# Tiles 4 to 8 of a pooled-attention and expert kernel in the form of the later tiles

## The chip, the cores and the metric

The kernel runs on one core of one Trainium2 chip. The metric is the device time of one execution in microseconds; the time before is the median of three runs. All engine times come from one profiled execution.

## The reference

Attention with pooled keys and values feeds a mixture of four experts. Batch is 8, heads 8, sequence 576, head size 64.

```python
k_p = k.reshape(B, H, Sp, 8, D).mean(axis=3)      # 576 rows -> 72
v_p = v.reshape(B, H, Sp, 8, D).mean(axis=3)
scores = scale * np.matmul(q, k_p.transpose(0, 1, 3, 2))
attn = exp(scores - max) / (sum + 1e-09)
x = np.matmul(attn, v_p)                          # -> x: 4608 tokens x 512
p = domain_probs / (domain_probs.sum(-1, keepdims=True) + 1e-09)
for e in range(4):
    out += p[:, e:e+1] * (np.maximum(x @ w1[e], 0.0) @ w2[e])   # 512 -> 1024 -> 512
```

## The kernel before

The 4608 tokens are 36 tiles of 128 tokens, and four tiles are a group. The expert part runs over 36 steps, one for each group and expert. A step has twelve slots. In every three slots there are two blocks of `up` (L807, a 128 x 512 product block of the next step, four products each, with a Relu on ScalarE) and one `down` (L843, one tile of this step, eight products, and `collect` on VectorE). `up` fills one of two `h_ps` banks, `down` one of two `o_ps` banks. Step 0 has only its last `down`, in slot 11; tiles 0 to 3 are prepared before slot 0 in an order written out by hand.

The attention of the later tiles is laid between these products. A dictionary `plan` holds, for a slot number counted through all steps, the functions that are called when the slot's products have been issued. Within an engine the order of the program is the order of the work. So this plan decides what each engine does next, and a wait at the head of an engine holds everything behind it.

Before the change the tiles come in two forms.

- **Tiles 4 to 8** (`plan_tile`): `gather_q` (L195) picks a tile's queries out of the wide load `qrun`; `turn_q` turns them with four 128 x 128 transposes on TensorE (L512); `scores` (L555) is four products against `kT`, in which the keys of a pair of heads lie beside blocks of zeros; `less_max` (VectorE) subtracts the row's maximum; `expo` (ScalarE) takes the exponential into `e_sb`; `normalise` (VectorE) divides; `turn_e` turns the probabilities with five transposes (L512); `context_turned` (L753) is eight products against `vblk`, in which the values are spread beside zeros.
- **Tiles 9 to 35** (`plan_pair`): queries and probabilities are turned on VectorE in blocks of 32; `scores_by_quarters` (L580) and `context_by_quarters` (L772) use products of 64 x 64, four of which address the four quarters of TensorE's array. These products are put into the middle of a `down`: the dictionary `parted` names the slots, and there six of eight products come first, then the block, then the last two.

Keys and values are folded from eight rows to one on VectorE (`fold_k`, `end_k`, `fold_v`, `end_v`). `WB = 2` says that batches 0 and 1 have the layout with zeros (`kTs`, `vblks`). From batch 2 on, `kTh` and `vh` hold them without zeros, and `spread_v` fills the part of `vh` that the last eight of a head's 72 rows need. Loads that convert to bf16 are issued on GpSimd (POOL), in program order, with eight semaphores in turn: an issue waits until the load eight before it has landed. Float32 loads and the output's stores are issued on SyncE (SP).

PSUM has two `ps_h` banks, two `ps_o` banks, one double bank `ps_s` (`sc`) and two `ps_t` banks for turns and contexts.

Of the kernel before, what the change touches and what calls it, by code (L numbers as in the profile page):

```python
# [10 lines left out]
ALU = mybir.AluOpType  # L11
# [6 lines left out]
def kernel(  # L18
# [33 lines left out]
    PW = 2 * SP  # L52

    WB = 2
# [62 lines left out]
    def load_k(b):  # L117
        if b < KB:
            load_rows(nc.gpsimd, kraw[b % 2], rows_of(k[b]))
            return  # L120

        n, mid = HR // 2, HR // 2 // BLK
        odd = n - mid * BLK
        for n32 in range(P // BLK):
            y, half = divmod(n32, 2)
            p0 = n32 * BLK
            for g in range(2):
                head = 4 * g + 2 * y
                rows = k[b][head:head + 2, :, half * BLK:(half + 1) * BLK].rearrange(
                    "z (j r) d -> (z j) r d", r=POOL  # L130
                )

                r = odd * g
                parts = [(r + a * BLK, r + (a + 1) * BLK) for a in range(mid)]
                parts.append((0, odd) if g else (n - odd, n))
                for r0, r1 in parts:
                    a, i = divmod(g * n + r0, BLK)
                    nc.gpsimd.dma_start(  # L138
                        out=k_blocks(b)[p0 + i:p0 + i + r1 - r0, a].rearrange(
                            "i (r d) -> i r d", d=BLK  # L140
                        ),
                        in_=rows[r0:r1],
                    )

    def load_v(b):
        if b < WB:
            load_rows(nc.gpsimd, vraw[b % 2], rows_of(v[b]))
            return


        if b < WB + 2:
            nc.gpsimd.memset(vraw[b % 2][0:TAIL, NB - 1, :], 0.0)
        rows = v[b].rearrange("(g y z) (j r) d -> g z j y (r d)", g=2, y=2, r=POOL)
        to = vraw[b % 2][:].rearrange("p (c y) x -> p c y x", y=2)
        for g in range(2):
            for z in range(2):
                p0 = g * D + z * REST
                nc.gpsimd.dma_start(out=to[g * D:(g + 1) * D, z], in_=rows[g, z, 0:D])  # L158
                nc.gpsimd.dma_start(out=to[p0:p0 + REST, 2], in_=rows[g, z, D:SP])  # L159
# [10 lines left out]

# [22 lines left out]
    def gather_q(t):  # L193
        qrow[t] = qpool.tile([P, NPAIR, 2, D], BF16, name="qrow")
        nc.vector.tensor_copy(  # L195
            out=qrow[t][:],
            in_=qrun[:, :, :, t - TPG - 1, :].rearrange("p z c d -> p c z d"),
        )

    def load_qblk(b):  # L200

        qblk[b] = qbpool.tile([P, NPAIR * (S // BLK), BLK], BF16, name="qblk")
        for n32 in range(P // BLK):
            y, half = divmod(n32, 2)
            to = qblk[b][n32 * BLK:(n32 + 1) * BLK].rearrange("i (g c) d -> i g c d", g=2)
            for g in range(2):
                head = 4 * g + 2 * y
                nc.gpsimd.dma_start(  # L208
                    out=to[:, g],
                    in_=q[b][head:head + 2, :, half * BLK:(half + 1) * BLK]  # L210
                    .rearrange("z (a i) d -> i (z a) d", i=BLK),
                )
# [63 lines left out]

    after(k0[0:1, 1, POOL * D - 1:POOL * D])
# [6 lines left out]
    load_q(TPG)  # L284
    load_w1(2, (0,))
    load_w2(1, halves)
    load_q_wide()
# [7 lines left out]
    vblks = [raw.tile([P, NB, NZ, D], BF16, name=f"vblk{i}") for i in range(2)]  # L295
    nc.scalar.memzero(vraw[0][TAIL:P, NB - 1, :])
    for t in (vraw[1], *kraw):
        nc.scalar.memzero(t[TAIL:P, NB - 1, :])
    kTs = [raw.tile([P, ROWS], BF16, name=f"kT{i}") for i in range(2)]
    for t in kTs:  # L300
        nc.scalar.memzero(t[:])
    for t in vblks:
        nc.scalar.memzero(t[:, :, 0])
# [87 lines left out]
    def turn_k(b):  # L391

        flat = pads[b][:].rearrange("p i z d -> p (i z d)")
        ps = ps_t.tile([P, NB * P], BF16, tag="t", name="kT_ps")
        for i in range(NB):

            nc.tensor.transpose(
                ps[:, i * P:(i + 1) * P], flat[:, i * P:(i + 1) * P], ident[:]
            )
        kT[b] = kTs[b % 2] if b < WB else kTh[b % 2]  # L400
        copy = nc.scalar.copy
        for z in range(2):
            half = slice(z * D, (z + 1) * D)
            if b >= WB:
                copy(
                    out=kT[b][half].rearrange("x (g r) -> x g r", g=2),
                    in_=ps[half, 0:ROWS].rearrange("x (g y r) -> x y g r", g=2, y=2)[:, z],
                )
                continue
            copy(  # L410
                out=kT[b][half].rearrange("x (c z j) -> x z c j", z=2, j=SP)[:, z],
                in_=ps[half, 0:ROWS].rearrange("x (z c j) -> x z c j", z=2, j=SP)[:, z],
            )
# [28 lines left out]
    def end_k0(*copies):  # L442
        kT[0] = kTs[0]
# [7 lines left out]
    vsum = {}  # L451

    def fold_v(b, n):
        fold(vraw[b % 2], 0, NB if b < WB else NB + 1, n)

    def end_v(b):
        rows = vraw[b % 2]
        if b >= WB:
            vblk[b] = vh[b % 2]
            nc.vector.tensor_add(  # L460
                out=vblk[b][:, 0:3].rearrange("p c y d -> p (c y) d"),
                in0=rows[:, :, 0:D], in1=rows[:, :, D:2 * D],
            )
            return
        vsum[b] = prep.tile([P, NB, D], BF16, name="v_sum")
        nc.vector.tensor_add(
            out=vsum[b][:], in0=rows[:, 0:NB, 0:D], in1=rows[:, 0:NB, D:2 * D]
        )

    def spread_v(b):  # L470
        if b >= WB:

            nc.vector.tensor_tensor(
                out=vblk[b][:, 3:5],
                in0=vblk[b][:, 2].unsqueeze(1).to_broadcast([P, 2, 2, D]),
                in1=mask_r[:].unsqueeze(2).to_broadcast([P, 2, 2, D]), op=ALU.mult,
            )
            return
        vblk[b] = vblks[b % 2]
        nc.vector.tensor_tensor(  # L480
            out=vblk[b][:, :, 1:NZ],
            in0=vsum[b][:].unsqueeze(2).to_broadcast([P, NB, MZ, D]),
            in1=mask_v[:], op=ALU.mult,
        )

# [10 lines left out]
    def spread_part(b, i0, i1):  # L496
        vblk[b] = vblks[b % 2]
# [63 lines left out]
    def scores_by_quarters(t, apart):  # L561


        if apart:

            banks = [ps_h.tile([P, 512], F32, tag="h", name="scq")[:] for _ in range(2)]
            ds[t] = soft.tile([P, 2, 4, SP], F32, name="d_sb")
        else:
# [3 lines left out]
        for pair in range(NPAIR):  # L572
            g, z = divmod(pair, 2)
            at = (2 * z + g) * SP
            for i in range(2):

                half, b = slice(i * D, (i + 1) * D), (t * P + i * D) // S
                for y in range(2):
                    dims = slice(y * D, (y + 1) * D)
                    nc.tensor.matmul(  # L580
                        banks[y][half, at:at + SP], lhsT=qT[t][dims, pair, half],
                        rhs=kT[b][dims, pair * SP:(pair + 1) * SP],
# [42 lines left out]
    def expo(t):  # L625
# [6 lines left out]
        if t >= DT:  # L632
# [21 lines left out]
    def normalise(t):  # L654
# [4 lines left out]
        if t >= DT:  # L659
# [100 lines left out]
    def context_by_quarters(tiles):  # L760
# [3 lines left out]
        banks = [ps_t.tile([P, n, 2, P], F32, tag="t", name="xT_ps") for _ in range(2)]  # L764
# [17 lines left out]
        for g in range(2):  # L782
            nc.scalar.copy(  # L783
                out=dst[:, 2 * g:2 * g + 2].rearrange("p y (c x) -> p y c x", c=n),
                in_=banks[g][:].rearrange("p c y x -> p y c x"),
            )

    def by_quarters(done, t, apart):

        if apart:  # L790
            scores_by_quarters(apart, True)
        if t:
            scores_by_quarters(t, False)
        if done:
            context_by_quarters(done)
# [115 lines left out]
    def plan_tile(t, base, steps):  # L911
        at(base, turn_q, t)
        at(base + steps[0], scores, t)
        at(base + steps[0], less_max, t)
        at(base + steps[1], expo, t)
        at(base + steps[2], normalise, t)
        at(base + steps[3], turn_e, t)
        at(base + steps[4], context_turned, t)
        return base + steps[4] + 1
# [4 lines left out]
    def plan_pair(slot, done, tiles, turns, second):  # L924

        parted[slot] = (done, tiles[0], tiles[1] if len(tiles) > 1 else None)
# [11 lines left out]
    plan_batch(1, 3, 4, 5, 7, 18, 19, 20, 21)  # L938
    for t in range(TPG, 2 * TPG):
        assert plan_tile(t, 12 + 3 * (t - TPG), (3, 5, 6, 9, 11)) <= 3 * SLOTS - 2  # L940
    for t in range(TPG + 1, DT):
        at(t + 8, gather_q, t)
    due = DT - 1 - TPG
    assert plan_tile(DT - 1, due * SLOTS - 14, (2, 4, 5, 8, 10)) <= due * SLOTS
    slot = due * SLOTS - 1
    plan_batch(2, *(slot + x for x in (-7, -6, -5, -3, 1, 2, 3, 4)))
    plan_pair(slot, [], [DT, DT + 1], (slot - 2, slot - 1), slot + 9)
# [15 lines left out]
    parted[(NT - 1 - TPG) * SLOTS - 4] = (done, None, None)  # L963
# [10 lines left out]
    for i in range(2):  # L974
        nc.scalar.memzero(vraw[i][:, NB, :])
# [91 lines left out]
    zeros = [x for i in range(2) for x in (ehalf[i][:, 2 * P:], eTh[i][:, 2])]  # L1067
    for i, x in enumerate(zeros):
        at(SLOTS + 3 * i + 2, nc.scalar.memzero, x)
# [5 lines left out]
    for s in range(NSTEP):  # L1075
        for slot in range(SLOTS):
# [6 lines left out]
            elif s > 0 or i == TPG - 1:  # L1083
                n = s * SLOTS + slot
                if n in parted:

                    down(s, i, 0, FB - 2)
                    by_quarters(*parted.pop(n))
                    down(s, i, FB - 2)
# [36 lines left out]
```

## Time and profile before

| | |
|---|---|
| median of three runs | 543.76 us (543.41 to 544.13) |
| profiled execution | 543.71 us |
| its span | 542.0 us |
| granted TensorE clock | 1.000 |
| TensorE busy | 534.3 us (99%), 3626 products |
| VectorE busy | 391.1 us (72%) |
| ScalarE busy | 236.2 us (44%) |
| GpSimd busy | 200.4 us (37%) |
| start of slot 0 | 32.12 us |
| start of the `down` of slot 47 | 88.00 us |

Busy times are shares of the whole span. In the timeline of an engine a line gives the start, the busy time, the engine, the source line, the operation, the tiles as out<-in, the part of the array, the shape and the count. Products are pipelined, so a group's busy time overlaps the next group's start; the difference of two starts is the time that a group takes on the engine.

### The profile page before, as it was taken

How to read it: one execution, taken by the hardware profiler on the slowest of the kernel's cores; microseconds unless marked ns; L12 is line 12 of the kernel's file. 1: busy time of each engine (PE TensorE's matmuls, PEld its weight loads, DVE VectorE, ACT ScalarE, POOL GpSimd, SP SyncE). 2: the span in 40 equal slices, each digit the busy share in tenths (PEclk: the TensorE clock that was granted, in tenths of full speed). 3: DMA queues.
4: the chain of work that ended last, by engine and by line, in shares of the span. 5: the costliest groups of instructions: out<-in, count | busy, mean ns of one | idle time of the engine just before them, and what ended most of it. 6: DMA issues, size and time to landing. Idle time of an engine off the chain costs nothing.

```text
span 542.0 us, 9291 instructions
## 1 busy us (share of the span) xinstructions
PE 534.3 (99%) x3626; PEld 258.4 (48%) x3626; DVE 391.1 (72%) x969; ACT 236.2 (44%) x423; POOL 200.4 (37%) x338
## 2 busy tenths in 40 slices
PE   7999999999999999999999999999999999999997
PEld 5754554444444444444444444444444444444444
DVE  5846846997979687888979797979797968522223
ACT  7444655344344444435344544354434444333330
POOL 6253299999996002991099422000000000000000
PEclk9999999999999999999999999999999999999999
DMA  9999999696979012793169949001000100011002
GB/s 228 207 201 205 191 109 106 35 56 33 113 47 88 2 46 38 29 58 61 59 26 41 68 88 37 0 1 59 21 0 1 59 21 0 2 39 40 0 1 78
DMA packets 135052, 33.78 MB, mean 62 GB/s; under 512 B 112544, under 2 KB 129952, under 8 KB 135008
## 3 DMA queue, kind: packets, MB, share of 16 engines
q0 software_dynamic: 122928, 21.45, 53.9%
q1 hardware_dynamic: 12080, 11.74, 6.7%
q8 instruction: 28, 0.46, 0.4%
q14 instruction: 16, 0.13, 0.1%
HBM read 45.16 MB, written 9.44 MB: 101 GB/s over the span
## 4 chain that ended last, share of the span: by engine, by line
PE 95%; DVE 2%; DMA 1%; ACT 1%; issue 1%; SPq 0%
PE o_ps L843 45%; PE h_ps L807 44%; PE h_ps L824 1%; PE xT_ps L772 1%; DMA qg<-in_q_dram 1%; PE scq L580 1%; PE xT_ps L753 0%; PE sc L580 0%; PE eT_ps L512 0%; PE last_ps L876 0%; PE sc L555 0%; DVE d_sb L606 0%; DVE ebuf L676 0%; SPq L109 0%; PE qT_ps L512 0%
## 5 line engine op out<-in xcount | busy, mean ns | idle before, releaser
L811 ACT ACTIVATE h_sb<-h_ps 128x512 bf16<-128x512 f32 x280 | 167.1, 597 | 247.3 <-PE h_ps L807 247.0
L843 PE MATMUL o_ps<-w,h_sb 128*128 128x512 bf16 x1144 | 272.4, 379 | 0.0
L807 PE MATMUL h_ps<-xT,w 128*128 128x512 bf16 x1120 | 265.7, 379 | 0.0
L843 PEld LDWEIGHTS <-h_sb 128*128 128x128 bf16 x1144 | 110.5, 98 | 131.8
L807 PEld LDWEIGHTS <-w 128*128 128x128 bf16 x1120 | 108.9, 98 | 128.5 <-issue 0.2
L858 DVE SCALAR_TENSOR_TENSOR acc<-o_ps,p_sb,acc 128x512 f32<-128x512 f32 x107 | 79.6, 744 | 84.3 <-PE o_ps L843 83.3
L138 POOL DMA_DIRECT2D kraw<-in_k_dram x200 | 111.3, 567 | 67.7 <-DVE khalf L383 40.9
L697 DVE STREAM_TRANSPOSE late<-late 32x96 f32<-32x96 f32 (+1 forms) x432 | 109.2, 253 | 6.8
L854 DVE TENSOR_SCALAR acc<-o_ps,p_sb 128x512 f32<-128x512 f32 x36 | 26.6, 740 | 40.9 <-PE o_ps L843 40.8
L208 POOL DMA_DIRECT2D qblk<-in_q_dram x48 | 38.8, 831 | 30.1 <-DVE qT L534 17.5
L671 DVE TENSOR_TENSOR late<-e_sb,rs 128x32 bf16<-128x32 f32 (+1 forms) x81 | 24.6, 369 | 0.9
L657 DVE TENSOR_REDUCE total<-e_sb 128x8 f32<-128x576 f32 x33 | 24.6, 745 | 0.6 <-ACT e_sb L638 0.3
L633 ACT ACTIVATE e_sb<-d_sb 128x576 f32<-128x576 f32 x27 | 18.4, 683 | 14.5 <-DVE d_sb L618 14.5
L534 DVE STREAM_TRANSPOSE qT<-qblk 128x512 bf16<-128x512 bf16 (+1 forms) x30 | 19.2, 650 | 0.2
L606 DVE TENSOR_TENSOR d_sb<-sc,mx 128x576 f32<-128x576 f32 x22 | 16.6, 756 | 0.7
L599 DVE TENSOR_REDUCE mx<-sc 128x8 f32<-128x576 f32 x22 | 16.4, 747 | 0.8 <-PE sc L555 0.7
L158 POOL DMA_DIRECT2D vraw<-in_v_dram x24 | 15.6, 648 | 1.9 <-DMA qblk<-in_q_dram 0.8
L783 ACT CAST xT<-xT_ps 128x512 bf16<-128x512 f32 (+1 forms) x28 | 14.8, 590 | 2.7 <-PE xT_ps L772 2.7
L159 POOL DMA_DIRECT2D vraw<-in_v_dram x24 | 15.0, 624 | 0.4 <-DMA qblk<-in_q_dram 0.2
L586 ACT COPY d_sb<-scq 128x288 f32<-128x288 f32 x26 | 9.1, 402 | 13.6 <-PE scq L580 13.6
L351 DVE TENSOR_TENSOR vraw<-vraw 128x1536 bf16<-128x1536 bf16 (+3 forms) x14 | 10.3, 737 | 0.2
L618 DVE TENSOR_TENSOR d_sb<-d_sb,mx 128x576 f32<-128x576 f32 x13 | 9.8, 757 | 0.4
(109 smaller groups left out, 220.8 us busy)
## 6 DMA issues: line engine op xcount, KB each, us to landing
out_dram<-acc SPq DMA_DIRECT2D x35, 256.0 KB, 2.0
w<-in_moe_w_dram POOLq DMA_DIRECT2D x12, 512.0 KB, 13.8
qblk<-in_q_dram POOLq DMA_DIRECT2D x48, 72.0 KB, 3.9
vraw<-in_v_dram POOLq DMA_DIRECT2D x24, 128.0 KB, 3.6
kraw<-in_k_dram POOLq DMA_DIRECT2D x160, 16.0 KB, 2.2
w<-in_moe_w_dram POOLq DMA_DIRECT2D x2, 1024.0 KB, 18.0
k<-in_k_dram SPq DMA_DIRECT2D x2, 512.0 KB, 4.0
qg<-in_q_dram SPq DMA_DIRECT2D x2, 512.0 KB, 6.5
```

The lines of the kernel that those rows point to most:

```text
L138: nc.gpsimd.dma_start(out=k_blocks(b)[p0 + i:p0 + i + r1 - r0, a].rearrange("i (r d) -> i r d", d=BLK), in_=rows[r0:r1],)
L208: nc.gpsimd.dma_start(out=to[:, g], in_=q[b][head:head + 2, :, half * BLK:(half + 1) * BLK] .rearrange("z (a i) d -> i (z a) d", i=BLK),)
L534: nc.vector.transpose(out=qT[t][:, :, at:at + n], in_=qblk[b][:].rearrange("p (c a) j -> p c (a j)", c=NPAIR)[:, :, tok:tok + n],)
L633: nc.scalar.activation(out=e, in_=ds.pop(t)[:].rearrange("p g h j -> p (g h j)"), func=ACT.Exp, scale=EXP_SCALE,)
L657: nc.vector.reduce_sum(out=total[:], in_=e, axis=AX.X)
L671: nc.vector.tensor_tensor(out=to, in0=e[:, s_, j_].rearrange("p s j y -> p s y j"), in1=rs[:, s_].unsqueeze(3).to_broadcast(list(to.shape) ...
L697: nc.vector.transpose(out=dst.rearrange("p (c k) -> p c k", k=P)[:, 0:n, toks], in_=src.rearrange("p (c k) -> p c k", k=P)[:, 0:n, rows],)
L807: nc.tensor.matmul(ps[:], lhsT=w1_sb[e][:, kc, fb * P:(fb + 1) * P], rhs=xT[g][:, kc, :], start=(kc == 0), stop=(kc == KC - 1),)
L811: nc.scalar.activation(out=hs[s][:, fb, :], in_=ps[:], func=ACT.Relu)
L843: nc.tensor.matmul(ps[:], lhsT=hs[s][:, fb, i * P:(i + 1) * P], rhs=w2_sb[e][:, fb, :], start=(fb == 0), stop=(fb == FB - 1),)
L854: nc.vector.tensor_scalar_mul(out=accs[t][:], in0=ps[:], scalar1=p_sb[:, e, t:t + 1])
L858: nc.vector.scalar_tensor_tensor(out=accs[t][:], in0=ps[:], scalar=p_sb[:, e, t:t + 1], in1=accs[t][:], op0=ALU.mult, op1=ALU.add,)
```

## The change

`WB` becomes 1: batch 1 is loaded and folded in the layout without zeros, and batch 0's values, once spread for tiles 0 to 3, are copied into that layout too (`move_v0`, 20 DMAs from SBUF to SBUF on SP, after one memzero on ScalarE). Heads are assigned to halves in another order from batch 1 on, which changes only indices. Tiles 4 to 8 then take the form by quarters:

- `turn_q_by_quarters`, slot 8: the queries of all five tiles in 80 transposes of 64 x 64, and four copies out of PSUM, two on ScalarE and two on VectorE. `gather_q` goes. `load_q_wide` is issued ahead of half of `load_w1(2)` and of `load_w2(1)`.
- Slot 11: scores of tiles 4 and 5. Slot 20: scores of 7, turns of the probabilities of 4 and 5 (`turn_e_by_quarters`, 48 transposes and four copies), scores of 6. Slot 29: scores of 8, turns of 6 and 7. Slot 32: contexts of 4 to 7, with copies on ScalarE and VectorE. Each block lies inside a `down`; a block can now stand after four products instead of six.
- Tile 8's probabilities are turned by six whole transposes in slot 40 (`turn_e_whole`), and its context joins the block that is in slot 47 already.
- The keys of batch 1 are folded in slots 0 to 2 and turned in slot 4 (before: 3 to 5, and 7); its values are folded in 18 and 19, ended in 24 and spread in 25 (before: 18 to 21).

The core of the diff (the text of `turn_e_whole`, the other places of the new indices and some allocations are left out):

```diff
-    WB = 2
+    WB = 1
...
     load_k(1)
     load_q(TPG)
+    load_q_wide()
     load_w1(2, (0,))
     load_w2(1, halves)
-    load_q_wide()
     load_w1(2, (1,))
     load_v(1)
...
+    def move_v0():
+        vblk[0] = vh[0]
+        nc.scalar.memzero(vh[0][:, 2])
+        for head in range(H):
+            y, g, z = head // NPAIR, head // 2 % 2, head % 2
+            r, end = head * SP, (head + 1) * SP
+            while r < end:
+                i, p = divmod(r, P)
+                j = r - head * SP
+                n = min(end - r, P - p, D - j if j < D else REST)
+                p1, c = (g * D + j, z) if j < D else (g * D + z * REST + j - D, 2)
+                nc.sync.dma_start(
+                    out=vh[0][p1:p1 + n, c, y, :],
+                    in_=vspread[p:p + n, i, head - 2 * i + 2, :],
+                )
+                r += n
...
+    def turn_q_by_quarters():
...
+        one = ps_s.tile([P, 2, 1024], BF16, name="sc")
+        four = [ps_t.tile([P, TPG, NPAIR, D], BF16, tag="t", name="qT_ps") for _ in range(2)]
+        for k in range(-1, TPG):
+            for c in range(NPAIR):
+                for i in range(2):
+                    half = slice(i * D, (i + 1) * D)
+                    for y in range(2):
+                        dims = slice(y * D, (y + 1) * D)
+                        if k < 0:
+                            to = one[dims, i, c * D:(c + 1) * D]
+                            src = qrow[TPG][half, c, y, :]
+                        else:
+                            to = four[i][dims, k, c, :]
+                            src = qrun[half, y, c, k, :]
+                        nc.tensor.transpose(to, src, ident[half, half])
+        for i, copy in enumerate((nc.scalar.copy, nc.vector.tensor_copy)):
+            half = slice(i * D, (i + 1) * D)
+            copy(
+                out=qT[TPG][:, :, half],
+                in_=one[:, i, 0:NPAIR * D].rearrange("p (c x) -> p c x", x=D),
+            )
+            copy(out=qwide[:, :, :, half], in_=four[i][:])
+
+    def turn_e_by_quarters(tiles):
+        banks = [ps_t.tile([P, len(tiles), 2, 3, D], BF16, tag="t", name="eT_ps")
+                 for _ in range(2)]
+        for n, t in enumerate(tiles):
...
+                            nc.tensor.transpose(
+                                banks[i][g * D:(g + 1) * D, n, y, c, :],
+                                ehalf[t % 2][half, r:r + D, y], ident[half, half],
+                            )
+        for n, t in enumerate(tiles):
+            for i, copy in enumerate((nc.scalar.copy, nc.vector.tensor_copy)):
+                copy(
+                    out=eT[t][:, :, i * D:(i + 1) * D, :].rearrange("p c x y -> p y c x"),
+                    in_=banks[i][:, n],
+                )
...
-    plan_batch(1, 3, 4, 5, 7, 18, 19, 20, 21)
-    for t in range(TPG, 2 * TPG):
-        assert plan_tile(t, 12 + 3 * (t - TPG), (3, 5, 6, 9, 11)) <= 3 * SLOTS - 2
-    for t in range(TPG + 1, DT):
-        at(t + 8, gather_q, t)
+    plan_batch(1, 0, 1, 2, 4, 18, 19, 24, 25)
+    at(1, move_v0)
+    at(8, turn_q_by_quarters)
+    parted[11] = (FB // 2, [
+        (scores_by_quarters, 4), (scores_by_quarters, 5, "t"), (less_max, 4),
+    ])
+    at(11, less_max, 5)
+    at(12, expo, 4)
+    at(13, normalise, 4)
+    at(13, expo, 5)
+    at(14, normalise, 5)
+    at(15, spread_v, 0)
+    parted[20] = (FB - 2, [
+        (scores_by_quarters, 7, "h"), (turn_e_by_quarters, [4, 5]),
+        (scores_by_quarters, 6), (less_max, 6),
+    ])
+    at(20, less_max, 7)
+    at(21, expo, 6)
+    at(22, normalise, 6)
+    at(24, expo, 7)
+    at(24, normalise, 7)
+    parted[29] = (FB // 2, [(scores_by_quarters, 8), (turn_e_by_quarters, [6, 7]), (less_max, 8)])
+    both = nc.scalar.copy, nc.vector.tensor_copy
+    parted[32] = (FB - 2, [
+        (context_by_quarters, [4, 5], "t", both), (context_by_quarters, [6, 7], "s", both),
+    ])
+    at(33, expo, 8)
+    at(34, normalise, 8)
+    at(40, turn_e_whole, 8)
...
-    assert plan_tile(DT - 1, due * SLOTS - 14, (2, 4, 5, 8, 10)) <= due * SLOTS
...
-    plan_pair(slot, [], [DT, DT + 1], (slot - 2, slot - 1), slot + 9)
+    plan_pair(slot, [DT - 1], [DT, DT + 1], (slot - 2, slot - 1), slot + 9)
...
-    zeros = [x for i in range(2) for x in (ehalf[i][:, 2 * P:], eTh[i][:, 2])]
-    for i, x in enumerate(zeros):
-        at(SLOTS + 3 * i + 2, nc.scalar.memzero, x)
+    for i in range(2):
+        at(i, nc.scalar.memzero, ehalf[i][:, 2 * P:])
```

## The prediction

> **What bounds the kernel now.** I read the page first, then the timeline of TensorE, where the start of a group minus the start of the next is what the group costs on the path, then DVE's timeline and the landing events.
>
> ```profile
> span 542.0 us, 9291 instructions
> ...
> PE 534.3 (99%) x3626; PEld 258.4 (48%) x3626; DVE 391.1 (72%) x969; ACT 236.2 (44%) x423; POOL 200.4 (37%) x338
> ...
> PE 95%; DVE 2%; DMA 1%; ACT 1%; issue 1%; SPq 0%
> ```
>
> Page, parts 1 and 4: TensorE is always busy and is 95% of the chain. It runs in program order, so each nanosecond taken out of its stream, or added by a wait, shows at the end. The granted clock is 1.000 over the span. The profiled execution took 543.71 us, 1.7 us of it outside the span; the median is 543.76, so a difference carries over as it is.
>
> ```profile
> 53.69 0.44 PE L512 MATMUL eT_ps<-ident,ebuf 128*128 128x128 bf16 x5
> 54.09 0.41 PE L555 MATMUL sc<-kT,qT 128*128 128x144 bf16 x4
> 54.34 0.39 PE L512 MATMUL qT_ps<-ident,qrow 128*128 128x128 bf16 x4
> 54.56 1.03 PE L807 MATMUL h_ps<-xT,w 128*128 128x512 bf16 x4
> ...
> 58.48 0.44 PE L512 MATMUL eT_ps<-ident,ebuf 128*128 128x128 bf16 x5
> 59.34 0.41 PE L555 MATMUL sc<-kT,qT 128*128 128x144 bf16 x4 [0.41 <-DVE d_sb L606]
> ...
> 66.36 0.61 PE L753 MATMUL xT_ps<-eT,vblk 128*128 128x128 bf16 x8
> 66.80 1.03 PE L807 MATMUL h_ps<-xT,w 128*128 128x512 bf16 x4
> ```
>
> TensorE's timeline, old form: a tile's scores cost 54.34-54.09 = 0.25, its turn of queries 0.22, its context 0.44. Five turns of probabilities are worth 5 x 55.8 ns = 0.28; at 58.48 they cost 0.86, a wait.
>
> ```profile
> 88.00 1.46 PE L843 MATMUL o_ps<-w,h_sb 128*128 128x512 bf16 x6
> 89.39 0.32 PE L580 MATMUL scq<-late,qT 64*64 64x72 bf16 x16
> 89.54 0.30 PE L580 MATMUL sc<-late,qT 64*64 64x72 bf16 x16
> 89.78 0.60 PE L843 MATMUL o_ps<-w,h_sb 128*128 128x512 bf16 x2
> 90.22 0.38 PE L807 MATMUL h_ps<-xT,w 128*128 128x512 bf16 x1
> ...
> 128.84 0.30 PE L580 MATMUL sc<-late,qT 64*64 64x72 bf16 x16
> 128.97 0.40 PE L772 MATMUL xT_ps<-late,vh 64*64 64x128 bf16 x16
> 129.30 0.60 PE L843 MATMUL o_ps<-w,h_sb 128*128 128x512 bf16 x2
> ```
>
> The same, later tiles' form. Six products at 215.8 ns end at 89.30; the block starts at 89.39, leaves at 89.78, and the two after it take 0.44 for 0.43: 0.49 in all. Scores in mid-block are 128.97-128.84 = 0.13 per tile (four quarters, 32.5 ns per four). So 0.49 - 2 x 0.13 = **0.23 per block** is entering and leaving. The 16 context products cost 0.33, of which 0.10 is leaving: 57 ns per four of 128 wide. In the block of 157.75 four 64 wide take 31 ns.
>
> **Removed from TensorE (tiles 4 to 8).** Turns of queries 5 x 0.22 = 1.13. Scores 0.38 + 4 x 0.25 = 1.38. Turns of probabilities 0.40 + 0.86 + 3 x 0.28 = 2.10. Contexts 0.47 + 4 x 0.45 = 2.25. One up product waits 0.09 for a bank at 44.74. Sum 6.95, some 0.9 of it waiting on DVE and ACT.
>
> **Added to TensorE.** Five blocks x 0.23 = 1.16. Scores 5 x 0.13 = 0.65. Turns of queries, 80 of 64 wide = 20 fours x 31 ns = 0.62. Turns of probabilities for tiles 4 to 7, 96 = 24 fours = 0.74. Contexts: tile 4 lies in two batches, 8 fours of 64 wide = 0.25; tiles 5 to 7, 12 fours x 57 = 0.68; tile 8 joins the block of slot 47, 4 fours and its end, 0.24. Tile 8's six whole turns, 6 x 55.8 = 0.34. Sum 4.68. **Difference -2.27 us**, 1.34 from fewer array cycles, 0.93 from waits that go.
>
> No row has a turn by quarters. Lower bound 27 ns per four (64 of the 128 columns that take 55.8, side by side), -0.2 in all; upper bound 4 x 27.9 ns if the quarters don't run side by side, +3.6. I take 31, the nearest row: same 64x64 loads, same 64 columns. The probabilities' loads read every second element, which no load here does; if that doubled 31 to 57 it costs 0.6.
>
> The Trainium skill speaks against this step (TensorE: Matmul & The Clock Gate, sections LDWEIGHTS and Weight-path perf modes): a load takes its columns / 1.2 GHz, and only full 128-column loads get the fast path. By it, as an estimate, a four waits 53 ns for its loads and the change brings 1.3 us instead of 2.3. The trace disagrees: the scores' loads have 64 columns too, and a four takes 32.5 ns.
>
> **What must arrive earlier.** The change pulls work forward, so I redid the engines' orders slot by slot with these durations.
> - Turns of queries, slot 8, TensorE at 37.6 (before's slot 9 starts at 37.61). They need `load_q_wide`, which landed at 43.59 behind `w2(1)`. The change moves it ahead of `w1(2)`'s first half, which landed at 35.85; so 35.9 to 36.3, over 1 us early. Moved past it, each 2.5 us later: `w1(2)` half, 38.5 for slot 12 at 42.4; `w2(1)`'s second half, 43.6 to 44.3 for 45.0 in slot 14. Cost 0, margin 0.7.
> - Batch 1's keys, three slots earlier: DVE ended them at 34.75; the turn comes at 35.6. ACT's three memzeros in slots 0 and 1 (0.30 each, row L1094) stand beside Relus that take 0.6 of each 0.86; the last ends at 35.0, and TensorE asks for that Relu's bank at 35.85.
> - `load_v(1)`: eight issues on POOL for two (0.6 each; what is queued behind there waits on landings anyway); last landing 49.05 becomes 49.5 to 52; DVE asks at 50.8.
> - `move_v0`: 20 small DMAs on SP from 35.0 on, when ACT's memzero in slot 1 is done; 0.43 to 0.5 each (SP's issues at the start), so 45, and 2.0 (output stores) to 6.2 (`dp1` under load) to land: 47 to 51. `spread_v(0)` waits for them on DVE, with the collects and `fold_v(1)` behind it; DVE gets there at 50.0. Cost 0. The 576 pieces over 16 engines at some 23 ns each delay the weights by under 0.9.
> - `load_k(3)` and `load_v(3)` change their slots, but POOL reaches them at 81 and 105 as before.
>
> ```profile
> 43.61 0.29 DVE L195 COPY qrow<-qrun 128x512 bf16<-128x512 bf16 x1 [1.60 <-DMA qrun<-in_q_dram]
> ```
>
> ```profile
> 48.00:60.00 12.00, 11.59 (x89) 6.39 (x88) 10.69 (x20) 6.55 (x14) 4.32 (x6) 1.00 1.24 207
> ```
>
> First line, DVE's timeline: today the first gather waits for the wide load. Second, a window: DVE (third pair) is busy 10.69 of 12 us, the nearest thing to a second bound. After, from 41.4 on, DVE has until the turns of tiles 6 and 7 (slot 29, TensorE at 63.2): four tiles' maxima and differences, 4 x 1.45; four normalisations in the other form (0.78+0.30+0.24+0.63+0.19 = 2.14), 8.6; five collects x 0.67 = 3.4; values of batches 0 and 1, 2.0; two copies out of PSUM, 0.7. Sum 20.5, so it ends at 61.9: margin 1.3. ACT's copies for the turns of queries (0.38, about 1.0 by 585 ns for 512 and 402 for 288) end at 39.6, scores follow at 41.1; ACT has room (6.55 of 12 us).
>
> I find no new wait on TensorE. Startup is unchanged, and so is all after slot 47.
>
> **The rivals.**
> - *DVE becomes the bound.* If its copies are dearer, or `load_v(1)` lands at 54, `expo` holds ACT, a Relu's bank comes late, and slot 29 waits: landing at 54 costs 1.8 by the same schedule, giving 543.2. For it: DVE's margin is 1.3 in 20. Against: the waits of before, with the same engine at 89%, cost only 0.9. Span: 542.7 to 544.8, no difference. Chance 0.14.
> - *Turns by quarters don't run side by side* (this one ends slower): at 27.9 ns each the 176 cost 4.91 for 1.36, +3.55, so 545.0. It decides from 83 ns per four. For it: no row shows it. Against: three kinds of quarter products all do run side by side. Chance 0.10.
> - *`move_v0` lands late*: 56 instead of 47 holds DVE in slot 15, its collect holds an output bank in slot 23 (1.7), ACT's bank in slot 25 (2.3), slot 29 (0.7): +4.7, so 546.1; from 54 on the gain is gone. For it: `dp0` kept SP for 2.83 and small DMAs took 6 us under load. Against: 3 us between 47 and DVE's arrival. Chance 0.10.
> - *The change does nothing*, because TensorE hides short products: excluded by the table, where every group moves the next start.
>
> **The numbers.** Forecast 543.7 - 2.3 = **541.4**, chance 0.66; its own range is 540.9 (loads at the lower bound, leaving cheaper) to 542.6 (strided loads 0.6, a wait of half a us). About 0.2% (1.1 us) is what a measurement can tell from no change: faster 0.66, same 0.14 (the DVE rival), slower 0.20 (the other two). The range reaches through the DVE rival: 540.8 to 544.5.
>
> **What would show it.** Right: slot 8's block costs 0.85, slot 47 starts 2.5 us earlier than at 88.00 and its block is 0.24 longer; no TensorE idle over 0.1 between 32 and 88; everything behind shifted by 2.3. Wrong: fours of turns above 40 ns; "DVE vh" waiting for a DMA on vh or vraw; h_ps starts spaced over 216 ns in slots 22 to 29; a turn of queries waiting for qrun.

## The result, and the profile after

Over 19 runs of each on the same chips the changed kernel takes a median of 545.23 us and the kernel before 543.60 us: ratio 1.0028, interval 1.0018 to 1.0039. That is 1.6 us slower where 2.3 us faster was forecast, and outside the range given. The runs of the changed kernel lie between 542.99 and 546.81, those of before between 543.03 and 544.84. Six runs of the changed kernel, at 545.33 to 546.62, show a mean granted clock of 0.995 to 0.997, where the profiled one shows 1.000. The profiled execution took 545.25 us against 543.71, so the account below has to explain +1.54 us.

The page of the changed kernel, parts 1, 4 and 5:

```profile
span 543.5 us, 9826 instructions
...
PE 532.4 (98%) x3867; PEld 255.8 (47%) x3867; DVE 394.9 (73%) x986; ACT 233.5 (43%) x417; POOL 203.4 (37%) x343
...
PE 70%; POOL 14%; DMA 14%; issue 1%; DVE 1%
...
L857 PE MATMUL h_ps<-xT,w 128*128 128x512 bf16 x1120 | 264.6, 379 | 2.2 <-ACT h_sb L861 2.2
```

TensorE is busy for 1.9 us less, as intended, but the span is 1.5 us longer. The chain of waits is 70% TensorE where it was 95%, but this does not point at the loss: the chain leaves TensorE at 158.48, at a wait of 0.25 us for queries turned on VectorE, which the kernel before has too (0.37 us at 157.47), and the faster late_spread below shows 71%. The last line shows the place: `up` products (L857) waited 2.2 us for a Relu.

TensorE's timeline after (start, busy, engine, line; a bracket gives idle time and what ended it). Lines are those of the changed kernel: turns of queries L566, of probabilities L587, scores L633, contexts L831, `up` L857, `down` L893.

```profile
35.89 1.89 PE L857 MATMUL h_ps<-xT,w 128*128 128x512 bf16 x8
37.71 0.32 PE L566 MATMUL sc<-ident,qrow 64*64 64x64 bf16 x16
37.85 0.80 PE L566 MATMUL qT_ps<-ident,qrun 64*64 64x64 bf16 x64
38.59 1.90 PE L857 MATMUL h_ps<-xT,w 128*128 128x512 bf16 x8
...
52.57 0.32 PE L633 MATMUL scq<-late,qg 64*64 64x72 bf16 x16
52.72 0.61 PE L587 MATMUL eT_ps<-ident,late 64*64 64x64 bf16 x48
53.15 0.32 PE L633 MATMUL sc<-late,qg 64*64 64x72 bf16 x16
...
57.30 1.03 PE L857 MATMUL h_ps<-xT,w 128*128 128x512 bf16 x4
60.50 1.02 PE L857 MATMUL h_ps<-xT,w 128*128 128x512 bf16 x4 [2.18 <-ACT h_sb L861]
61.36 1.89 PE L893 MATMUL o_ps<-w,h_sb 128*128 128x512 bf16 x8
...
65.92 0.36 PE L587 MATMUL eT_ps<-ident,late 64*64 64x64 bf16 x24
66.64 0.50 PE L587 MATMUL eT_ps<-ident,late 64*64 64x64 bf16 x24 [0.36 <-DVE late L724]
```

The new blocks themselves are cheap: 80 turns of queries fit between 37.71 and 38.59. But the eight `up` products that begin at 57.30 last until 61.36, 4.07 us where eight take 1.73: **2.34 us of waiting in slot 25**. In slot 29 the turns of tiles 6 and 7 stop for VectorE's normalisation (L724) in three gaps that together cost **0.67 us**; the largest, at 66.64, is in brackets.

VectorE's timeline after shows where this begins:

```profile
49.37 0.91 DVE L724 TENSOR_TENSOR late<-e_sb,rs 128x512 bf16<-128x512 f32 x3
54.45 0.29 DVE L447 TENSOR_TENSOR vh<-vh,mask_r 128x256 bf16<-128x256 bf16 x1 [4.16 <-issue]
54.65 0.75 DVE L908 SCALAR_TENSOR_TENSOR acc<-o_ps,p_sb,acc 128x512 f32<-128x512 f32 x1
55.31 1.54 DVE L343 TENSOR_TENSOR vraw<-vraw 128x1536 bf16<-128x1536 bf16 x2
56.77 1.05 DVE L593 COPY qg<-eT_ps 128x384 bf16<-128x384 bf16 x2
57.71 0.75 DVE L652 TENSOR_REDUCE mx<-sc 128x8 f32<-128x576 f32 x1
58.49 0.76 DVE L659 TENSOR_TENSOR d_sb<-sc,mx 128x576 f32<-128x576 f32 x1
```

VectorE reaches `spread_v(0)` (L447) at 50.3 and stands still for 4.16 us. The profile calls the releaser "issue", because it does not name a transfer there; the landing events of `move_v0`'s copies do: the last landed at 54.27. Behind it in VectorE's program order are a collect, `fold_v`, the copies of the turned probabilities and tile 6's maximum and difference, which is done only at 59.2.

ScalarE's timeline carries it on to TensorE:

```profile
54.91 0.60 ACT L861 ACTIVATE h_sb<-h_ps 128x512 bf16<-128x512 f32 x1 [0.25 <-PE h_ps L857]
59.28 0.68 ACT L686 ACTIVATE e_sb<-d_sb 128x576 f32<-128x576 f32 x1 [3.78 <-DVE d_sb L659]
59.87 1.06 ACT L861 ACTIVATE h_sb<-h_ps 128x512 bf16<-128x512 f32 x2
```

`expo(6)` stands at the head of ScalarE's queue and waits 3.78 us for VectorE's difference. The Relus behind it (59.87) are what would free TensorE's `h_ps` banks; TensorE's second four products can start only then. So one late copy on SP passes through VectorE and ScalarE to TensorE.

The copies themselves, by their source line (busy least/median/most in ns, first and last start in us):

```profile
L465 SPq DMA_DIRECT2D vh<-vspread x20: 515/643/810, 14.6 to 48.5; - x20
```

The account of the profiled executions, before to after, where a block's cost is the distance between the two neighbouring groups less the 1.727 us of eight products:

| term | us |
|---|---|
| predicted difference of TensorE's work | -2.27 |
| wait in slot 25 | +2.34 |
| wait in slot 29 | +0.67 |
| blocks dearer than predicted (slot 8 0.98 for 0.85; 20 0.93 for 0.86; 32 1.33 for 1.16; others within 0.02) | +0.35 |
| longer end of the program | +0.46 |
| sum (measured +1.54) | +1.55 |

The longer end: from the landing of the last store to the end of the execution 0.98 us pass before and 1.44 us after. SP ends by waiting for the semaphores of its DMA queues one after the other in a fixed order. Stores use eight of them in turn; the 20 additional DMAs (20 is 4 more than a multiple of 8) move the last three stores from late places in that order to early ones, so that the rest of the list is still to be gone through when they land. That is 0.25 us of the 0.46: from the last landing to the end of the list 0.39 us pass instead of 0.14. The other 0.22 us lie behind the list, where VectorE's last drain comes later (543.20, when ScalarE's and TensorE's came at 542.8 to 542.9); rest_first, with the same order of stores, does not have them, and their cause stays open.

### The profile page after: what moved, and what is told of

It is laid out like the page before. It is cut to its first block, busy times and chain, and to the rows that moved or that the text cites. A ratio compares the mean times of both kernels' runs of the same rounds, so it can differ in the third digit from the quotient of the medians.

```text
span 543.5 us, 9826 instructions
## 1 busy us (share of the span) xinstructions
PE 532.4 (98%) x3867; PEld 255.8 (47%) x3867; DVE 394.9 (73%) x986; ACT 233.5 (43%) x417; POOL 203.4 (37%) x343
## 4 chain that ended last, share of the span: by engine, by line
PE 70%; POOL 14%; DMA 14%; issue 1%; DVE 1%
PE o_ps L893 35%; PE h_ps L857 33%; POOL kraw L139 9%; DMA kraw<-in_k_dram 9%; DMA w<-in_moe_w_dram 2%; DMA qblk<-in_q_dram 2%; PE xT_ps L831 1%; POOL vraw L159 1%; POOL vraw L160 1%; POOL qblk L201 1%; POOL w L217 1%; POOL w L210 1%; DMA k<-in_k_dram 1%; PE scq L633 1%; PE last_ps L926 0%
## 5 line engine op out<-in xcount | busy, mean ns | idle before, releaser
L893 PE MATMUL o_ps<-w,h_sb 128*128 128x512 bf16 x1144 | 273.1, 379 | 0.0
L857 PE MATMUL h_ps<-xT,w 128*128 128x512 bf16 x1120 | 264.6, 379 | 2.2 <-ACT h_sb L861 2.2
L857 PEld LDWEIGHTS <-w 128*128 128x128 bf16 x1120 | 109.4, 98 | 133.7 <-issue 2.5
L893 PEld LDWEIGHTS <-h_sb 128*128 128x128 bf16 x1144 | 110.2, 98 | 131.2
L908 DVE SCALAR_TENSOR_TENSOR acc<-o_ps,p_sb,acc 128x512 f32<-128x512 f32 x107 | 79.6, 744 | 78.1 <-PE o_ps L893 77.1
L724 DVE TENSOR_TENSOR late<-e_sb,rs 128x32 bf16<-128x32 f32 (+1 forms) x96 | 29.2, 370 | 1.2
L686 ACT ACTIVATE e_sb<-d_sb 128x576 f32<-128x576 f32 x32 | 21.8, 683 | 18.7 <-DVE d_sb L671 14.8
L159 POOL DMA_DIRECT2D vraw<-in_v_dram x28 | 18.1, 646 | 5.0 <-DMA w<-in_moe_w_dram 3.6
L160 POOL DMA_DIRECT2D vraw<-in_v_dram x28 | 17.7, 634 | 5.0 <-DMA w<-in_moe_w_dram 4.1
L842 ACT CAST xT<-xT_ps 128x512 bf16<-128x512 f32 (+1 forms) x31 | 16.1, 579 | 4.2 <-PE xT_ps L831 4.2
L652 DVE TENSOR_REDUCE mx<-sc 128x8 f32<-128x576 f32 x20 | 14.9, 747 | 2.1 <-PE sc L633 2.0
L659 DVE TENSOR_TENSOR d_sb<-sc,mx 128x576 f32<-128x576 f32 x20 | 15.1, 756 | 0.6
L343 DVE TENSOR_TENSOR vraw<-vraw 128x1536 bf16<-128x1536 bf16 (+1 forms) x14 | 10.5, 753 | 0.2
```

The costliest lines, as they stand in the source:

```text
L724: nc.vector.tensor_tensor(out=to, in0=e[:, s_, j_].rearrange("p s j y -> p s y j"), in1=rs[:, s_].unsqueeze(3).to_broadcast(list(to.shape) ...
L857: nc.tensor.matmul(ps[:], lhsT=w1_sb[e][:, kc, fb * P:(fb + 1) * P], rhs=xT[g][:, kc, :], start=(kc == 0), stop=(kc == KC - 1),)
L893: nc.tensor.matmul(ps[:], lhsT=hs[s][:, fb, i * P:(i + 1) * P], rhs=w2_sb[e][:, fb, :], start=(fb == 0), stop=(fb == FB - 1),)
L908: nc.vector.scalar_tensor_tensor(out=accs[t][:], in0=ps[:], scalar=p_sb[:, e, t:t + 1], in1=accs[t][:], op0=ALU.mult, op1=ALU.add,)
```

## The experiments

The theory: `move_v0`'s copies land too late, and through VectorE and ScalarE this costs the 3.0 us of waits (where an expectation uses letters, L). The rival (F) is that the loss does not hang on this landing, so that moving `spread_v(0)` would not bring the forecast gain. All kernels below are the changed kernel with one edit or, towards the end, two or three, except the last, which is the kernel before with one; each was timed against the kernel before on the same chip.

| kernel | median us (range, runs) | ratio to before | interval | TensorE's last product ends |
|---|---|---|---|---|
| before, after | 543.60, 545.23 | 1.0028 | 1.0018-1.0039 | 538.81, 539.85 |
| late_spread | 542.25 (542.20-542.46, 8) | 0.9973 | 0.9963-0.9983 | 536.86 |
| rest_first | 542.11 (541.86-542.36, 6) | 0.9970 | 0.9959-0.9982 | 537.17 |
| no_moves | 541.88 (541.61-541.92, 5) | 0.9964 | 0.9952-0.9977 | 536.50 |
| early_moves | 542.13 (542.06-542.30, 7) | 0.9970 | 0.9959-0.9981 | 536.73 |
| expo_later | 545.15 (543.43-545.64, 11) | 1.0024 | 1.0015-1.0033 | 539.75 |
| more_moves | 549.59 (549.25-550.04, 4) | 1.0111 | 1.0097-1.0125 | 544.13 |
| rest_first_24 | 541.75 (541.60-541.98, 5) | 0.9967 | 0.9954-0.9979 | 536.90 |
| early_24 | 542.01 (541.80-543.06, 9) | 0.9972 | 0.9962-0.9982 | 537.09 |
| waits_early | 541.70 (541.59-542.10, 5) | 0.9965 | 0.9952-0.9977 | 536.60 |
| before_later | 543.90 (543.66-544.03, 11) | 1.0005 | 0.9996-1.0014 | 539.02 |

**late_spread: let VectorE ask later.** Only the call of `spread_v(0)` moves; the 20 copies stay.

```diff
-    at(15, spread_v, 0)
+    at(30, spread_v, 0)
```

> The changed kernel, but spread_v(0) is called in slot 30 instead of 15; nothing else is moved. Theory L (the 20 small DMAs land at 54 us and spread_v(0) holds VectorE for them, which costs TensorE 2.34 us in slots 24 and 25 and 0.72 in slot 29): VectorE never waits, both stalls go, the median falls by about 3.0 to 542.2, and TensorE reaches slot 47 at 85.8 instead of 88.9. Rival F (VectorE is full, its queue is late without the DMAs too): VectorE still reaches slot 29's probabilities late, a stall of 1 us or more stays, 543.5 or slower.

Measured 542.25. Both waits are gone. VectorE goes from the normalisation through the collect to `fold_v` without a stop:

```profile
49.24 0.91 DVE L724 TENSOR_TENSOR late<-e_sb,rs 128x512 bf16<-128x512 f32 x3
50.07 0.74 DVE L908 SCALAR_TENSOR_TENSOR acc<-o_ps,p_sb,acc 128x512 f32<-128x512 f32 x1
50.73 1.54 DVE L343 TENSOR_TENSOR vraw<-vraw 128x1536 bf16<-128x1536 bf16 x2
```

The same turns, the same copies and the same weights behind them cost 3 us less on TensorE when VectorE does not stand before them. This bears out the theory and speaks against the rival. The copies land no earlier, the last at 55.20, only nobody stands waiting. The spread of the runs also shrinks, from 3.8 us to 0.3 us; that the landing is what varied from run to run fits this, but only one execution of each kernel has a trace.

**rest_first: let the pieces that are asked for land first.** `spread_v` needs only the eight pieces of eight rows with `c` equal to 2; the others are read by the contexts in slot 32.

```diff
-                nc.sync.dma_start(out=vh[0][p1:p1 + n, c, y, :], in_=vspread[...])
+                pieces.append((c != 2, vh[0][p1:p1 + n, c, y, :], vspread[...]))
...
+        for _, to, src in sorted(pieces, key=lambda x: x[0]):
+            nc.sync.dma_start(out=to, in_=src)
```

> The changed kernel, spread_v(0) in slot 15 as it is, but move_v0 issues the eight 8-row pieces first, the only ones that spread_v(0) reads. Theory L: they land by 46 us, before VectorE gets there at 50, so the same 3.0 us as with the late call, 542.2. Rival F: no gain. If the wait is for the whole queue and not for these pieces, VectorE's wait of 4.2 us stays and so does 545.2.

Measured 542.11; the order of issue alone brings 3.1 us against the changed kernel. The eight pieces have landed by 44.33, and VectorE does not wait:

```profile
50.09 0.28 DVE L447 TENSOR_TENSOR vh<-vh,mask_r 128x256 bf16<-128x256 bf16 x1
50.29 0.74 DVE L909 SCALAR_TENSOR_TENSOR acc<-o_ps,p_sb,acc 128x512 f32<-128x512 f32 x1
```

**no_moves: what the copies cost beside the wait.** A memzero on ScalarE stands in place of the 20 DMAs, so batch 0's values are missing from the tokens of tile 4 that belong to it.

```diff
-        for head in range(H):
-            ...
-                nc.sync.dma_start(...)
+        nc.scalar.memzero(vh[0][:, 0:2])
```

> The changed kernel without the 20 DMAs: a ScalarE memzero fills their place, so batch 0's values are left out of the tokens of tile 4 that belong to it. Theory L: what the DMAs cost is the wait alone, so this equals the late call within 0.3 us, 542.2. Rival M (their 576 small pieces also slow the weights beside them and with them TensorE): at least 0.5 us faster than the late call.

Measured 541.88, only 0.23 to 0.37 us below the three kernels that keep 20 copies but do not wait for them. Two differences in the traces are enough for that: the end of the program takes 0.97 us instead of 1.44 (late_spread, early_moves) or 1.22 (rest_first), and the block in slot 32 costs 1.17 instead of 1.28 us, because TensorE has no DMA to wait for in it. So no cost is left over for the copies' traffic itself.

**early_moves: issue all copies earlier.** The memzero goes to ScalarE's first ones and `move_v0()` stands right behind the spreading of batch 0's values in the start; SP then issues from 14.64 to 28.1.

```diff
+    nc.scalar.memzero(vh[0][:, 2])        # among the first ones
...
+    move_v0()                              # after spread_part(0, 2, NB)
...
-    at(1, move_v0)
+    at(1, vblk.__setitem__, 0, vh[0])
```

> The changed kernel with the DMAs issued as soon as batch 0's values are spread (15 us) instead of in slot 1, their memzero among the first ones of ScalarE. Theory L: landed by about 30 us, no wait on VectorE, 542.2, unless they delay w2(0), which landed at 23.6 for a product at 24.4: then up to 1 us is given back in the startup.

Measured 542.13. SP spends the same 0.71 us per copy there, so this price is not one of the busy stage around 40 us. Nothing at the start became later.

**expo_later: take ScalarE out of the chain.** If `expo(6)` stands behind slot 22's Relus, the `h_ps` banks come free although VectorE is late.

```diff
-    at(21, expo, 6)
+    at(22, expo, 6)
```

> The changed kernel, with expo(6) called in slot 22 instead of 21, so that the Relu of slot 22 stands ahead of it on ScalarE. Theory L (VectorE is late as a whole; ScalarE only passes it on): the wait of 2.34 us before slot 25's up product goes, but the turns of tiles 6 and 7 in slot 29 wait some 3.0 us instead of 0.72; median unchanged, 544.9 to 545.3. Rival A (ScalarE's order is the cause): 2.3 us faster, 542.9.

Measured 545.15, the changed kernel's time. The expectation saw the rest of the wait in slot 29 alone; it went to three places, in TensorE's timeline:

```profile
59.96 1.89 PE L893 MATMUL o_ps<-w,h_sb 128*128 128x512 bf16 x8 [0.85 <-DVE acc L908]
...
64.48 1.02 PE L893 MATMUL o_ps<-w,h_sb 128*128 128x512 bf16 x4 [0.79 <-DVE acc L908]
...
66.61 0.50 PE L587 MATMUL eT_ps<-ident,late 64*64 64x64 bf16 x24 [0.66 <-DVE late L724]
```

Now collects (L908) come late and hold the output banks. ScalarE was only the path by which VectorE's lateness came to TensorE; another path costs as much. The plan has no slack between 50 and 67 us in which VectorE could make up the time.

**more_moves: make the landing later still.** Eight further copies of eight rows, into a tile that nothing reads, behind head 0's pieces.

```diff
+            for x in range(8 if head == 1 else 0):
+                nc.sync.dma_start(
+                    out=spare[8 * x:8 * x + 8, :], in_=vspread[8 * x:8 * x + 8, 0, 2, :]
+                )
```

> The changed kernel with eight more 8-row DMAs into an unused tile after the first two pieces, so the rest is issued some 8 x 0.65 = 5.2 us later and lands near 59.5 instead of 54.3. Theory L, by the slot schedule: from 54 on each us of landing costs TensorE one us; slot 23's product of the down block waits too; 550.3. If the landing isn't what VectorE waits for: 545.2.

Measured 549.59. VectorE and TensorE:

```profile
59.17 0.29 DVE L448 TENSOR_TENSOR vh<-vh,mask_r 128x256 bf16<-128x256 bf16 x1 [9.14 <-issue]
```

```profile
60.18 3.57 PE L898 MATMUL o_ps<-w,h_sb 128*128 128x512 bf16 x8 [4.57 <-DVE acc L913]
```

`spread_v(0)` starts 4.72 us later than in the changed kernel, TensorE's last product ends 4.28 us later, and the median rises by 4.4. So the landing is what VectorE waits for. But that each microsecond of landing costs one was not shown in the way expected. TensorE's waits between slots 20 and 30 are 4.9 us instead of 3.0. Around the end of the long wait the granted clock (the first number behind POOL's) is half for 6.8 us, from 58.71 to 65.53, and the 16 products of these two groups take 6.1 us instead of 3.5:

```profile
52.00:55.00 3.00, 3.00 (x91) 1.61 (x89) 0.00 (x0) 1.89 (x5) 2.17 (x3) 1.00 1.16 174
59.00:65.00 6.00, 4.82 (x12) 1.78 (x12) 5.76 (x10) 1.00 (x2) 1.62 (x2) 0.50 1.24 207
```

The slow products gave VectorE and ScalarE time to catch up; what slots 25 and 29 would have waited at the full clock can't be read from this run. That the sum came near the expected 550.3 is in part luck.

**rest_first_24 and early_24: mend the end of the program.** With the 64-row pieces in two halves there are 24 copies, a multiple of eight, so the last stores get their old semaphores back.

```diff
+                cuts = (0, 32, 64) if n == D else (0, n)
+                for a, b in zip(cuts, cuts[1:]):
...                  one copy for rows a to b
```

> The kernel with the 8-row pieces first, with each of the four 64-row pieces issued in two halves, so 24 DMAs instead of 20. Theory E (the last wait list on SP goes through its eight queue semaphores in a fixed order, and 20 more DMAs turn the last three stores from its end to its middle, so the end comes 1.44 us after the last landing instead of 0.98; 24 turn them by a whole round): the time from the last landing to the end is 0.98 again and the median falls by 0.4 to 541.7. Rival: the tail differs by chance, or four more issues cost time: 542.1 to 542.3.

> The same 24 DMAs issued early, at 15 us. Theory E: 542.13 of the early issue less 0.4 to 0.5, so 541.7. Rival: 542.1.

Measured 541.75 and 542.01. In both the end of the program takes 0.98 and 0.97 us again: the list ends 0.14 us after the last landing, which shows the cause of that part of the term, and VectorE's last drain is not late. The end had taken 1.22 us in rest_first and 1.44 in early_moves, so 0.24 and 0.47 could be gained; the medians fall by 0.36 and 0.12. TensorE's timeline of rest_first_24 shows what the four further copies cost:

```profile
66.56 1.46 PE L896 MATMUL o_ps<-w,h_sb 128*128 128x512 bf16 x6
67.94 1.03 PE L834 MATMUL xT_ps<-qg,vh 64*64 64x64 bf16 x48
68.80 0.64 PE L834 MATMUL sc<-late,vh 64*64 64x128 bf16 x32
69.37 0.60 PE L896 MATMUL o_ps<-w,h_sb 128*128 128x512 bf16 x2
```

The contexts of slot 32 read more pieces that were written by DMAs, and each further semaphore is a wait instruction on TensorE. All these copies landed long before, yet there are gaps of 105, 125 and 125 ns among the short products, where rest_first has one of 105: the block costs 1.52 instead of 1.28 us.

**waits_early: put these waits where long products hide them.** rest_first_24, and in slot 30, among long products, two products of two columns that read the moved values, into a tile that nothing reads.

```diff
+    def touch_v0():
+        ps = ps_t.tile([P, 2, 2], F32, tag="t", name="touch_ps")
+        for c in range(2):
+            nc.tensor.matmul(
+                ps[:, c], lhsT=vh[0][:, c].rearrange("p y d -> p (y d)"), rhs=zero[:, 0:2]
+            )
...
+    at(30, touch_v0)
```

> The kernel with 24 DMAs and the 8-row pieces first, and two products of two columns in slot 30 that read the moved values and whose result nobody uses. Theory W (each further wait for a DMA queue that stands on TensorE's sequencer among the short products of the block in slot 32 costs some 0.12 us there, although the DMA has long landed; ahead of long products it costs nothing): the products take these waits beside slot 30's long ones, the gaps of 105, 125 and 125 ns in the block go, the block of slot 32 costs 1.17 instead of 1.52, the two products cost 0.1, and the median falls from 541.75 to 541.5. Rival: the gaps are the array's and stay; 541.85.

Measured 541.70, the lowest median, though its range overlaps that of rest_first_24: 0.9965 of the kernel before (0.9952 to 0.9977), and 3.5 us below the changed kernel. TensorE's timeline:

```profile
66.58 1.46 PE L903 MATMUL o_ps<-w,h_sb 128*128 128x512 bf16 x6
67.97 0.69 PE L841 MATMUL xT_ps<-qg,vh 64*64 64x64 bf16 x48
68.48 0.63 PE L841 MATMUL sc<-late,vh 64*64 64x128 bf16 x32
69.04 0.61 PE L903 MATMUL o_ps<-w,h_sb 128*128 128x512 bf16 x2
```

The 48 context products are through in 0.51 us (68.48 - 67.97) instead of 0.86, the block costs 1.18 us, and the two extra products 0.06. TensorE's last product ends 0.30 us earlier, but the median falls only from 541.75 to 541.70, where 541.5 was expected. The two profiled executions also differ elsewhere: slot 0 of rest_first_24 starts 0.53 us earlier, and in slot 26 it waits 0.57 us, for the second half of `w2(2)` that landed at 59.72. What takes up the gain in the other runs was not settled.

**before_later: are the waits of the old form removable without the new one?** The kernel before, with the last two steps of tiles 4 to 8 one slot later.

```diff
-        assert plan_tile(t, 12 + 3 * (t - TPG), (3, 5, 6, 9, 11)) <= 3 * SLOTS - 2
+        assert plan_tile(t, 12 + 3 * (t - TPG), (3, 5, 6, 10, 12)) <= 3 * SLOTS - 2
```

> The kernel before, with turn_e and context_turned of tiles 4 to 7 called one slot later (steps 10 and 12 instead of 9 and 11). Theory S (0.7 of the 0.93 us of waits that the change takes from TensorE are turns of probabilities called too early for VectorE, and need no new form): the waits of 0.12 and 0.58 go, 543.0 to 543.2. Rival: VectorE is the bound there and the wait moves to the next step, 543.7.

Measured 543.90, no difference (0.9996 to 1.0014). TensorE's timeline:

```profile
53.93 0.41 PE L555 MATMUL sc<-kT,qT 128*128 128x144 bf16 x4 [0.23 <-DVE d_sb L606]
...
59.18 0.41 PE L555 MATMUL sc<-kT,qT 128*128 128x144 bf16 x4 [0.42 <-DVE d_sb L606]
```

The turns are no longer called ahead of the scores, and the scores still wait: by the starts 0.40 us at 53.93 and 0.60 us at 59.18, where before it was 0.12 at 54.09 and 0.58 at 59.34. So it is not the turns that waited but the scores behind them, for VectorE's difference (L606), which reads the `sc` bank that they write. This shift does not remove the waits counted in the prediction's "removed" sum; another plan of the old form that would was not tried.

## Why the prediction was wrong, and where it was right

**The step that failed: "`move_v0`: 20 small DMAs ... Cost 0."** It had three numbers. The start, 35.0, was right: 19 of the 20 issues begin at 34.85. The price of an issue, 0.43 to 0.5 us, came from SP's loads from DRAM at the start; measured are 0.76 us on average from one issue to the next, 0.72 without the longest (median busy 0.643; pieces of eight rows are mostly 0.62 to 0.65, pieces of 64 are 0.52), and one issue, at 47.69, began 1.48 us after the one before: the copy of 41.45, eight issues earlier on the same semaphore, had landed only at 47.67. So the last went out at 48.50 and not at 45. The time to land, 2.0 to 6.2 us, held: 3.3 to 6.2 were measured. But the cost of nothing came from the early end of that range, 47; its own late end, 45 + 6.2 = 51.2, was already behind VectorE's arrival at 50.0. With the measured issues the two ends are 50.5 and 54.7, and 54.27 it was. Had the last copy gone out at 45, the 5.8 us that it took would have meant a landing at 50.8, about half a microsecond behind VectorE; so most of the 4.16 us comes from the price of the issues.

The Trainium skill (DMA: Bandwidth & Descriptors, section "Anatomy of one DMA — SWDGE (gpsimd) path") gives about 2.0 us as the fixed time of one DMA issued on GpSimd, nearly constant. These copies are issued on SP, of which that section does not speak; if its figure held for them, as an estimate, the last piece would have landed at 50.5 and VectorE would have waited 0.4 us. Measured were 3.3 to 6.2 us beside the loads of weights, and 5.1 us for the first one, issued at 14.64 and landed at 19.72.

**The rival that occurred was the one with this mechanism, at too small a chance.** "From 54 on the gain is gone" was right. Its waits were priced for a landing at 56: 1.7 in slot 23, 2.3 in slot 25, 0.7 in slot 29. Measured with 54.27: none, 2.34 and 0.67. With 58.99, in more_moves, slot 23 waits 4.74 us, which is the rival's 1.7 and the 3 us by which the landing is later; but slots 25 and 29 wait only 0.1 us in all, and 2.6 us go to the slower clock, which the prediction did not have. A chance of 0.10 was too small for a step with 3 us of cover at an uncertainty of the landing that was itself 4 us wide, with 20 times an issue price taken from another kind of DMA on top.

**TensorE's own work was right to some tenths.** Forecast -2.27 us; where VectorE does not wait, TensorE's last product ends 1.64 (rest_first) to 2.31 us (no_moves) earlier than before. Term by term:

- Turns by quarters do run side by side, and the rival against it falls. The first 47 products of a block take 31 to 32 ns per four, the value taken from the scores. After that it is 33.5 ns, with gaps of 25 to 75 ns, in slot 8: 0.98 us for 0.85 (0.89 or 0.90 in most of the other kernels, which have fewer gaps). By the rule of the Trainium skill that the prediction weighed (TensorE: Matmul & The Clock Gate, section LDWEIGHTS), 53 ns per four, the 20 fours would take, as an estimate, 1.06 us by themselves and the block about 1.3; the trace disagrees here too.
- Loads of every second element cost nothing: in slot 20 the first 31 turns of probabilities go at 31 ns per four, as with dense loads.
- Slot 32 was mis-sized: 1.33 for 1.16 us. The term left out was TensorE's waits for the moved pieces; with these waits elsewhere (waits_early) it is 1.18, without them (no_moves) 1.17.
- Slot 11 (0.49), the whole turns in slot 40 (0.34 forecast, 0.335 measured) and tile 8's context in slot 47 (0.24, 0.23) were right.

**The other arrivals were right or slightly early.** `load_q_wide` landed at 35.49 (forecast 35.9 to 36.3), and the turn of queries did not wait. The last piece of `load_v(1)` landed at 49.33 (49.5 to 52), and VectorE came to `spread_v(0)` at 50.1 to 50.3 (50.0). VectorE's margin at slot 29 was 0.75 to 1.0 us without the wait (forecast 1.3). VectorE as the bound by itself did not occur.

**"Startup is unchanged, and so is all after slot 47" was wrong by 0.46 us,** the end of the program, in the changed kernel. Where the copies land in time, as in rest_first, the new form gives 542.1, which is 0.7 above the forecast of 541.4. In rest_first's trace the end takes 0.24 us more than before, the blocks of slots 8, 20 and 32 are 0.04, 0.07 and 0.11 dearer than forecast, slot 0 starts 0.11 us later, and two waits, in slot 26 and behind 154.94, are each 0.11 longer than before.

**One reading of the profile before was wrong.** The prediction books the 0.58 us at 58.48 as a wait of turns of probabilities. The bracket in its own lines stands at the scores of 59.34, and before_later shows that the scores wait for VectorE's difference. The sum of what goes is the same.

## What to carry to other kernels

A step that is moved or added on a quiet queue is not free because the queue is quiet: its landing has to be compared, at the late end of its range, with the moment at which an engine with other work behind the wait will ask for it. Sort such copies by who asks first; here the order of 20 issues alone was worth 3 us. And when an engine in the middle passes a delay on, taking it out of the chain may only move the wait to the next resource, as in expo_later; here the cause lay at the first idle gap in time, not at the engine whose idle time shows at the end.

## What the runs showed of the hardware that was not expected

- Copies from SBUF to SBUF of 8 to 64 rows issued on SP cost it 0.72 us each where none waits for an earlier landing; busy 0.52 for 64 rows, mostly 0.62 to 0.65 for eight, 0.73 to 0.81 for 24, 40 and 56. In the changed kernel landing takes 3.3 to 6.2 us beside the weights. Why it takes this long was not tested.
- A wait on TensorE for a DMA that landed long ago is not free: the wait instructions take 51 ns each, some 125 ns apart, and among quarter products they cost about 0.12 us each. Among long products they cost nothing that shows.
- Which semaphores the last stores use decides whether 0.14 or 0.39 us pass between the last landing and the end of SP's list of waits. In these kernels the number of DMAs on SP, taken modulo eight, sets it.
- When TensorE had stood still for 4.57 us (more_moves), its granted clock was 0.50 from 58.71 to 65.53, and products of 512 columns started 427 ns apart instead of 216. Behind the 2.18 us of the changed kernel's profiled execution the clock stayed at 1.00.
- More than some 47 quarter products in a row go on at 33.5 ns per four instead of 31 to 32, with gaps. Why was not tested.
- In the changed kernel GpSimd issues nine loads between 46.8 and 53.7. Among them the second half of `w2(2)` goes out at 48.34 (before: 38.74) and lands at 58.58, up to 60.0 in the kernels made from it, where it was 56.70 before. It is the next thing that would be late; what sets its landing was not tested.
